# Attention, expert layer and MLP in one kernel: the short query chunk moved to the front, the start script rearranged, and its value products split into column halves

## The chip, the cores and the metric

The kernel runs on one core of one Trainium2 chip. The metric is the device time of one execution in microseconds. The time before is 407.12 us, the median of three runs (406.49 to 407.96).

The engines are called TensorE (PE in the rows; its weight loads are PEld), VectorE (DVE), ScalarE (ACT), GpSimd (POOL) and SyncE (SP), whose queue issues nearly all transfers.

## The reference

Three stages follow one another. The change touches only the first.

```python
scores = scale * np.matmul(q, k.transpose(0, 1, 3, 2))        # B=2, H=8, S=576, D=64
x = (psi_rel / psi_i)[..., None]                              # log-distance over log-position
bias = np.maximum(x @ w1 + b1, 0.0) @ w2                      # 32 hidden, one bias per head
attn = softmax(scores + bias.transpose(2, 0, 1)[None])
x = np.matmul(attn, v)                                        # to 1152 x 512 tokens
# then: top-1 mixture of 8 experts (512 -> 1024 -> 512) with a capacity,
# then: an MLP 512 -> 2048 -> 512 with a leaky ReLU
```

The bias depends on the position pair and the head, not on the batch.

## The kernel before, in words

**Chunks and units.** The 576 queries of a batch are cut into five chunks, 0 to 3 of 128 queries and chunk 4, the short one, of 64. A *unit* is one chunk of one batch for one pair of heads, so there are 40 units. `order` (L573) lists the ten (batch, chunk) pairs, and the units follow it, four head pairs each. Before, the first is (0, 1), chunk 1 of batch 0; the short chunk of batch 0 is the fifth.

In a full unit the two heads are two score tiles of 128 queries by 576 keys. In a short unit they share one: rows 0 to 63 are the one head, rows 64 to 127 the other.

**Bias groups.** The bias is made in 36 groups of 16 query rows. For a group, `relus` (L156) makes four ReLU tiles of D columns, D = max(16u + 16, 576 - 16u) for group u. Each goes to an engine by the letter that `RENG` (L62), picked by the digit in `RP` (L63), gives: D VectorE, A ScalarE, P GpSimd. `bias_mm` (L172) multiplies them by the second layer on TensorE, and evicts from PSUM with a scale: groups with D over 512 come in two pieces, the first evicted by VectorE and the second by ScalarE; the others in one piece, on the engine that `EP` (L64) names (1 is ScalarE). The result is stored to a scratch tensor in DRAM (`scr`), mirrored for both sides of the diagonal. `load_bias` (L300) reads a unit's bias back, shifted row by row. Groups are made in the order in which the chunks first appear in `order`. Chunk 2 has the narrowest groups (D 304 to 384), chunks 0 and 4 the widest (up to 576). `do_bias` (L593) makes the next group and then the ReLUs of the group two further on.

**The start script.** `START` (L58) is a list of words. `START[0]` is run first, then the ReLUs of two groups, and then, for each further entry, one bias group, its store, and the entry's words (L627 to L633). The words: Q loads the queries of the first or second chunk, q splits one pair's queries into a high and a low part, k loads the keys of a head pair, K splits them, v loads a part of the values, B loads biases up to a unit. Before, twelve groups are made before the first unit, and B3 stands behind the eighth. All loads go through the SP queue, which works in order; a bias load there waits until the stores of its chunk have landed. The keys of pairs 2 and 3 are split in `prep` (L645) of units 0 and 1: ScalarE casts, and by `KHE` (L61) GpSimd subtracts.

**The main loop** (L1265) runs iteration n as follows: scores of unit n+1 (`qk`, TensorE), transposes of unit n (`tr`), score reduction with the bias for unit n+1 (`ttr`, VectorE, once for each score tile), evictions of the transposes, exponentials of unit n+1 (`expo`, ScalarE), `prep` of later queries and keys, one bias group, the finishing steps of a chunk, value products of unit n-1 (`pv`, TensorE, L391), more bias groups, and bias loads up to unit n+5. `QUOTA` (L70) says how many groups iteration n makes: two in iterations 0 to 9, then one, so the last of 36 is made in iteration 13. The score tile has one buffer, the ReLU tiles of a group three. `PF` (L69) says in which iterations a piece of the sorted-token buffer is pre-filled (six transfers of 771 KB), and batch 1's keys are split in iterations 8 to 10, with a subtraction on VectorE (`k_late`, L273).

**Value products.** `pv` gives for each of five key tiles, in a full unit, one product per head: 64 weight columns (the head's values) by 128 moving columns (the queries), each written to its own 64 rows of the output. In a short unit it gives one product for both heads: 128 weight columns by 128 moving columns, of which the finishing step reads the two diagonal 64 by 64 blocks. Every float32 product appears in the trace as two matmul passes.

The expert stage and the MLP start when attention has ended. The main loop's order, cut:

```python
    for n in range(N + 1):
        if n + 1 < N:
            st = s0(n + 1)
        if n < N:
            tt = tr(units[n][1], At.pop(n))
        if n + 1 < N:
            sv = ttr(*units[n + 1][1:], st, bts[n + 1])
...
            At[n + 1] = expo(c, p, sv, rst[b, c])
            prep(n + 1)
        q = quota[n]
        if q:
            do_bias()
...
            pv(c, p, ATt.pop(n - 1), Vt[b], xpt[b, c])
...
        for _ in range(q - 1):
            do_bias()
```

## Time and profile before

| | us |
|---|---|
| median of three runs | 407.12 |
| the profiled execution | 408.05 |
| its span, first to last instruction | 406.3 |
| TensorE busy | 375.9 |
| VectorE busy | 307.7 |
| ScalarE busy | 242.9 |
| GpSimd busy | 139.1 |

The profiled execution took 408.05 us, of which 406.3 are its span. Attention fills about the first 210 us, the expert stage and the MLP the rest. In a timeline row stand the start in us, the time in us, the engine, the line, the operation with the tiles it writes and reads, the shape, and in brackets how long the engine was idle before it and what ended that. Rows of one kind that follow one another are merged (x8 is eight). A matmul's end is modelled, so the cost of a step on TensorE is read from its start to the start of the next row.

### The profile page before, as it was taken

To read this page: it belongs to the slowest core of one execution; us is meant where nothing else is said; L and a number is where in the kernel's file an instruction comes from. 1 tells how busy PE (TensorE), PEld (TensorE's weight loads), DVE (VectorE), ACT (ScalarE), POOL (GpSimd) and SP (SyncE) were. 2 spreads that over 40 slices of the span, in tenths; PEclk is the share of its full clock that TensorE was granted. 3 is DMA by queue.
4 is the path that set the end of the run, shared out by engine and by line. 5 is a ranking of instruction groups with operands and counts; after the bars stand their busy time and mean duration, and the time that the engine had idled before them with its cause. 6 is when DMAs were issued, how large, how long until landed. Compare 5 with 4: busy or idle time off the path is not lost. (4 is left out here: it accounts for less than half of the span.)

```text
span 406.3 us, 8427 instructions
## 1 busy us (share of the span) xinstructions
PE 375.9 (93%) x2990; PEld 312.6 (77%) x2990; DVE 307.7 (76%) x733; ACT 242.9 (60%) x522; POOL 139.1 (34%) x110
## 2 busy tenths in 40 slices
PE   4777999988999999999999999999999999899993
PEld 2234666756688888988889999998988778788872
DVE  5998989899854888899458972137899999999310
ACT  3857898788865878767654875556544222455100
POOL 1445857574101110212332206840242255222311
PEclk9999899999999999999998999999999999999997
DMA  7979599798879938889185299683243366530011
GB/s 180 320 235 322 157 330 313 274 297 250 216 236 262 353 135 233 224 253 250 46 236 201 69 327 343 217 289 114 106 173 127 106 207 206 209 106 2 19 59 51
DMA packets 34050, 81.79 MB, mean 201 GB/s; under 512 B 8427, under 2 KB 8811, under 8 KB 31952
## 3 DMA queue, kind: packets, MB, share of 16 engines
q1 hardware_dynamic: 32880, 78.70, 61.3%
q0 software_dynamic: 1120, 2.48, 1.7%
q8 instruction: 25, 0.41, 0.4%
q14 instruction: 25, 0.20, 0.2%
HBM read 59.11 MB, written 23.20 MB: 203 GB/s over the span
## 5 line engine op out<-in xcount | busy, mean ns | idle before, releaser
L341 DVE CUSTOM_DVE_ANT_0 sv<-St,bt 128x576 f32<-128x576 f32 x72 | 52.9, 750 | 30.8 <-PE St L329 18.8
L672 POOL TENSOR_TENSOR P<-raw,P 128x1024 fp32r<-128x1024 f32 x18 | 45.3, 2521 | 76.6 <-ACT P L671 63.5
L352 ACT ACTIVATE A<-sv,mx 128x576 f32<-128x576 f32 x72 | 59.3, 837 | 3.2 <-DVE mx L341 3.0
L329 PE MATMUL St<-K,Q 128*128 128x320 f32 (+1 forms) x320 | 53.6, 310 | 2.6 <-DVE mx L341 2.2
L329 PEld LDWEIGHTS St<-K,Q 128*128 128x128 f32 x320 | 43.9, 189 | 14.6 <-issue 8.4
L182 PE MATMUL pb<-Gt,WP 128*32 128x272 f32 (+17 forms) x352 | 42.1, 505 | 13.3 <-DVE Gt L165 7.5
L269 POOL TENSOR_TENSOR Q<-qr,Q 128x256 fp32r<-128x256 f32 x22 | 16.9, 769 | 99.9 <-ACT Q L261 62.1
L165 DVE TENSOR_SCALAR Gt<-WL,bp 128x400 f32<-128x400 f32 (+17 forms) x98 | 49.4, 563 | 0.1
L671 ACT CAST P<-raw 128x1024 fp32r<-128x1024 f32 x27 | 28.3, 1048 | 28.3 <-DVE raw L689 22.7
L362 PE MATMUL pt<-CS,A 128*128 128x128 f32 x288 | 41.5, 284 | 1.3 <-ACT A L352 0.8
L372 ACT COPY AT<-pt 128x512 f32<-128x512 f32 x40 | 23.3, 583 | 29.2 <-PE pt L362 28.9
L362 PEld LDWEIGHTS pt<-CS,A 128*128 128x128 f32 x288 | 38.1, 206 | 2.2 <-ACT A L352 1.3
L169 POOL TENSOR_SCALAR Gt<-WL,bp 128x528 f32<-128x528 f32 (+12 forms) x17 | 34.1, 2009 | 8.2 <-DVE Gt L165 7.3
L399 PE MATMUL xp<-AT,V 128*64 128x128 f32 x512 | 35.9, 284 | 0.0
L399 PEld LDWEIGHTS xp<-AT,V 128*64 128x64 f32 x512 | 28.0, 139 | 9.8 <-issue 9.5
L182 PEld LDWEIGHTS pb<-Gt,WP 128*32 128x32 f32 x352 | 12.4, 110 | 29.8 <-DVE Gt L165 14.7
L856 PE MATMUL g<-yhl,P 128*128 128x304 f32 x96 | 30.5, 318 | 3.9 <-DVE gfa L881 3.9
L193 ACT ACTIVATE bs<-pb,CS 128x288 f32<-128x288 f32 (+53 forms) x60 | 27.2, 500 | 10.1 <-PE pb L182 9.5
L1193 PE MATMUL ac<-P,hq 128*128 128x512 f32 (+1 forms) x80 | 31.5, 394 | 0.0
L1191 PE MATMUL ac<-P,hq 128*128 128x512 f32 (+1 forms) x80 | 31.5, 394 | 0.0
L1192 PE MATMUL ac<-P,hq 128*128 128x512 f32 (+1 forms) x80 | 31.5, 394 | 0.0
L889 DVE TENSOR_TENSOR hq<-gfa,hq 128x304 fp32r<-128x304 f32 x32 | 28.9, 902 | 1.4 <-ACT hq L888 1.4
(322 smaller groups left out, 907.4 us busy)
## 6 DMA issues: line engine op xcount, KB each, us to landing
bt<-scr SPq DMA_DIRECT2D x24, 576.0 KB, 6.0
w<-wo SPq DMA_DIRECT2D x13, 1024.0 KB, 5.0
scr<-bs SPq DMA_DIRECT2D x36, 295.5 KB, 4.2
raw<-wm SPq DMA_DIRECT2D x14, 512.0 KB, 6.2
w<-wm SPq DMA_DIRECT2D x10, 512.0 KB, 5.7
srt<-pre SPq DMA_DIRECT2D x6, 771.0 KB, 8.4
qr<-qc SPq DMA_DIRECT2D x16, 256.0 KB, 5.7
w64g<-wo SPq DMA_DIRECT2D x3, 1024.0 KB, 10.3
```

The costliest lines, as they stand in the source:

```text
L165: nc.vector.tensor_scalar(G, src, bp[:, g : g + 1], 0.0, op0=ALU.add, op1=ALU.max)
L169: nc.gpsimd.tensor_scalar(G, src, bp[:, g : g + 1], 0.0, op0=ALU.add, op1=ALU.max)
L182: nc.tensor.matmul(pb[32 * q : 32 * q + 32, 0 : hi - lo], W2, gs[:, q, lo:hi], start=True, stop=True)
L329: nc.tensor.matmul(St[:, o + lo : o + hi], Q[:, h - 2 * p, w, :], K[:, h - 2 * p, lo:hi], start=n == 0, stop=n == len(seq) - 1)
L341: nc.vector.tensor_tensor_reduce(out=sv, in0=St, in1=bt[:, jb], scale=-0.125, scalar=3.0e38, op0=ALU.add, op1=ALU.min, accum_out=mx)
L352: nc.scalar.activation(A[:, :, j], sv, AF.Exp, bias=mx, scale=-1.0, accum_out=rs[:, col : col + 1])
L362: nc.tensor.transpose(pt[:, 128 * t : 128 * t + 128], A[:, 128 * t : 128 * t + 128, j], ident)
L399: nc.tensor.matmul(xp[64 * j : 64 * j + 64, p, :], w, a, start=t == 0, stop=t == NFULL)
L672: eng.tensor_tensor(out=P_[:, 1], in0=raw, in1=P_[:, 0].bitcast(F32), op=ALU.subtract)
L1191: nc.tensor.matmul(ps, hh, wh, start=k == 0, stop=False)
L1192: nc.tensor.matmul(ps, hh, wl, start=False, stop=False)
L1193: nc.tensor.matmul(ps, hl, wh, start=False, stop=k == F2 // 128 - 1)
```

## The change

Six constants change, and two pieces of code:

- `order` begins with the short chunk, (0, 4), then (0, 2) and (0, 1). The bias groups follow: chunk 4 (four groups), 2, 1, 3, 0. Batch 1 still begins at unit 12.
- `START` makes eight groups instead of twelve, with the queries of both first chunks and the keys 0 and 1 loaded before the first; B3 stands behind the fourth group, the values and the keys 2 and 3 behind B3.
- `QUOTA` makes three groups in iterations 0 and 1 and two in each of 2 to 12, so the last is made in iteration 12.
- `RP`, `RENG`, `EP` put ReLUs and evictions of some groups on other engines: VectorE has 99 ReLUs instead of 98, ScalarE 29 as before, GpSimd 16 instead of 17.
- `PF` moves the first four pre-fills to iterations 8, 11, 14 and 17 (before 1, 3, 8 and 14).
- In `pv`, a short unit's product is made per head, 64 weight columns by that head's 64 moving columns.

```diff
-START = ["Q0 k0 k1", "q0 v0", "q1 K0 v1", "q2", "Q1 q3 v2", "", "K1", "k2", "v3 B3 k3", "", "", "", ""]
+START = ["Q0 k0 k1 Q1", "", "q0", "K0 q1", "B3 q2 q3 k2", "K1 v0 v1", "v2 v3 k3", "", ""]
-RENG = ('DAAA', 'DADD', 'DAPD', 'DDDD', 'DDPA', 'DDAD')
-RP = "355355535352525234144534444144444342"
-EP = "111111111100011111111101110111111111"
+RENG = ('DAAA', 'DADD', 'DAPD', 'DDDD', 'DDPA', 'DDAD', 'DADA')
+RP = "565633533353525234144534444144444342"
+EP = "111111111111111111111101110111111111"
-PF = (3, 8, 1, 14, 21, 28)
-QUOTA = [2, 2, 2, 2, 2, 2, 2, 2, 2, 2, 1, 1, 1, 1, 1, 1, 1, 1, 1, 1, 1, 1, 1, 1, 2, 2, 1, 1]
+PF = (8, 11, 14, 17, 21, 28)
+QUOTA = [3, 3] + [2] * 11
...
-            for t in range(NFULL):
-                nc.tensor.matmul(xp[:, p, :], V[:, t, 128 * p : 128 * p + 128], AT[:, 0, 128 * t : 128 * t + 128],
-                                 start=t == 0, stop=False)
-            nc.tensor.matmul(xp[:, p, :], vt[:, 128 * p : 128 * p + 128], AX_[0:64], start=False, stop=True)
+            for t in range(NFULL + 1):
+                for j in range(2):
+                    r = slice(64 * j, 64 * j + 64)
+                    h = slice(128 * p + 64 * j, 128 * p + 64 * j + 64)
+                    w, a = (V[:, t, h], AT[:, 0, 128 * t + 64 * j : 128 * t + 64 * j + 64]) if t < NFULL else (vt[:, h], AX_[0:64, r])
+                    nc.tensor.matmul(xp[r, p, r], w, a, start=t == 0, stop=t == NFULL)
...
-    order = [(0, 1), (0, 0), (0, 3), (1, 3), (0, 4), (0, 2), (1, 2), (1, 1), (1, 0), (1, 4)]
+    order = [(0, 4), (0, 2), (0, 1), (1, 1), (0, 3), (0, 0), (1, 0), (1, 3), (1, 2), (1, 4)]
```

## Rows read from the trace of the kernel before

**Rows 1.** Busy us by stretch: PE, PEld, DVE, ACT, POOL; clock, DMA share, GB/s.

```profile
10.00:20.00 10.00, 7.53 (x44) 2.18 (x37) 9.91 (x20) 8.89 (x19) 4.47 (x4) 1.00 1.02 319
...
40.00:50.00 10.00, 9.96 (x90) 5.83 (x90) 9.96 (x24) 8.33 (x20) 8.84 (x14) 0.83 0.50 155
```

**Rows 2.** Timeline of TensorE, a full unit: scores, transposes, value products, next scores.

```profile
165.89 1.34 PE L329 MATMUL St<-K,Q 128*128 128x320 f32 x8
167.07 1.11 PE L362 MATMUL pt<-CS,A 128*128 128x128 f32 x8
...
168.22 1.09 PE L399 MATMUL xp<-AT,V 128*64 128x128 f32 x16
169.14 0.39 PE L399 MATMUL xp<-AX__2356,vd 128*64 128x128 f32 x4
169.46 1.33 PE L329 MATMUL St<-K,Q 128*128 128x320 f32 x8
```

**Rows 3.** Timeline of TensorE, a unit of the short chunk.

```profile
131.22 1.32 PE L329 MATMUL St<-K,Q 128*128 128x320 f32 x8
132.38 0.63 PE L362 MATMUL pt<-CS,A 128*128 128x128 f32 x4
...
132.95 1.06 PE L402 MATMUL xp<-AT,V 128*128 128x128 f32 x8
...
134.39 1.29 PE L329 MATMUL St<-K,Q 128*128 128x320 f32 x8
```

**Rows 4.** Timeline of TensorE, a wide and a narrow bias group, each with its successor.

```profile
63.09 1.04 PE L182 MATMUL pb<-Gt,WP 128*32 128x496 f32 x8
64.05 0.66 PE L436 MATMUL px<-CS,xt 128*128 128x128 f32 x4
...
83.36 0.72 PE L182 MATMUL pb<-Gt,WP 128*32 128x304 f32 x8
84.01 1.34 PE L329 MATMUL St<-K,Q 128*128 128x320 f32 x8
```

**Rows 5.** Timelines: the first score reduction on VectorE; scores of unit 3 on TensorE.

```profile
29.54 0.74 DVE L341 CUSTOM_DVE_ANT_0 sv<-St,bt 128x576 f32<-128x576 f32 x1
...
44.77 1.34 PE L329 MATMUL St<-K,Q 128*128 128x320 f32 x8
```

**Rows 6.** Timeline of the start: the load of keys 3 and its use on ScalarE.

```profile
28.17 0.50 SPq L226 DMA_DIRECT2D kr<-kc  x1
...
37.46 1.15 ACT L235 CAST K<-kr 64x1152 fp32r<-64x1152 f32 x1 [2.28 <-DMA kr<-kc]
```

**Rows 7.** Timelines: ReLUs on VectorE, alone and beside GpSimd's key subtraction.

```profile
4.85 1.54 DVE L165 TENSOR_SCALAR Gt<-WL,bp 128x448 f32<-128x448 f32 x4
...
79.10 0.66 DVE L165 TENSOR_SCALAR Gt<-WL,bp 128x320 f32<-128x320 f32 x2
...
12.10 1.54 DVE L165 TENSOR_SCALAR Gt<-WL,bp 128x368 f32<-128x368 f32 x1
...
12.00 2.90 POOL L238 TENSOR_TENSOR K<-kr,K 64x576 fp32r<-64x576 f32 x2 [0.25 <-POOL Q L269]
```

**Rows 8.** Timeline of the SP queue: last store of the first chunk, its bias loads.

```profile
21.03 0.32 SPq L222 DMA_DIRECT2D scr<-bs  x1
...
25.21 2.86 SPq L310 DMA_DIRECT2D bt<-scr  x4
```

**Rows 9.** Timeline of TensorE: router products with 64 moving columns, and their successor.

```profile
141.31 0.32 PE L444 MATMUL pl<-xt,WP 128*32 128x64 f32 x8
141.56 1.09 PE L399 MATMUL xp<-AT,V 128*64 128x128 f32 x16
```

**Rows 10.** Timelines: a late TensorE hole, key subtractions of batch 1, evictions of a wide group.

```profile
87.72 0.72 PE L182 MATMUL pb<-Gt,WP 128*32 128x304 f32 x8 [1.30 <-ACT bs L193]
...
93.17 2.62 DVE L276 TENSOR_TENSOR K<-kr,K 64x1152 fp32r<-64x1152 f32 x2
...
79.68 0.65 DVE L195 TENSOR_SCALAR bs<-pb,CS 128x16 f32<-128x16 f32 x2
```

## The prediction

> **What bounds the kernel now.** I read the busy shares by stretch first, then TensorE's timeline, then the timelines of the other engines where TensorE has holes.
>
> By stretch: between 10 and 20 us VectorE is full and TensorE is not; between 40 and 50 us TensorE is full, at a granted clock of 0.83 on average [rows 1]. "Full" has to be checked, because a matmul's end is modelled. What does not lie is the distance from one start to the next. A full attention unit costs TensorE 1.18 us of scores, 1.15 of transposes and 1.24 of value products, in all 3.57 us [rows 2]. A unit of the short chunk costs 1.16 + 0.57 + 1.44 = 3.17 us [rows 3]. A bias group of width D costs 0.96 us at 496 columns and 0.65 at 304 [rows 4], so 0.16 + 0.0016 D.
>
> With these prices I count packed work. The first score reduction starts on VectorE at 29.54 us and the scores of unit 3 on TensorE at 44.77 [rows 5]. By then TensorE has done 16 bias groups (widths summing to 7296: 14.2 us), scores of three units (3.5), transposes of two (2.3), products of one (1.2): 21.3 us of work in 44.8, so 23.5 us are lost. From there to 111 us, where the last bias group ends, the same count leaves only about 4 us lost, all after 86 us, and from there to the end of attention nearly nothing. So the question for the change is **when TensorE becomes packed, how much work is then left, and whether it stays packed.**
>
> Why it starts late: VectorE works through the ReLUs of 14 bias groups before the first score reduction, and then ScalarE stands still for 2.28 us for the keys of pair 3, whose load was issued at 28.17 and used at 37.46, 9.3 us later [rows 6]. While it stands, bias evictions and ScalarE's ReLUs queue behind that key cast, and TensorE behind them.
>
> **The change part by part.**
>
> *Eight groups ahead, four of them for the first chunk.* By the strings, VectorE does 33 ReLUs before the first reduction instead of 44. One costs 0.37 us at 448 columns and 0.29 at 320 [rows 7], so 11 fewer are about 4.4 us: the first reduction moves from 29.5 to about 25. Its bias must be there too. The four wide groups need on VectorE 10 wide ReLUs (4.2 us), 4 narrow ones (1.2), 4 evictions of about 0.6 (2.4) and the split of one query pair, which I take at 0.6; from 4.85 that is 13.3 us. K0's subtraction on GpSimd falls into this: a ReLU beside it took 1.54 us instead of about 0.33 [rows 7], so 14.5. The last store of the old first chunk was issued at 21.03, and the bias load, which waits for its landing, at 25.21 [rows 8]; with the same 4.2 us the bias load goes out at 18.7 and the data is there by about 23. VectorE is later, so 25 stands.
>
> *Key loads.* Keys 0 and 1 stay where they were; the second chunk's queries move ahead of everything (two issues on SP at a moment when nothing waits, and a memset of the short queries on GpSimd, idle then: I cost these at nothing; if that cover went, the first store would be some 2 us later, 2 us of start). Keys 2 and 3 are behind the bias load on SP. The four issues of it took 2.86 us [rows 8], then come keys 2, two stores, seven issues of values, and keys 3: ten issues at about half a microsecond, so keys 3 go out near 26.5, two us earlier than before. When they land is the unknown: after 4.2 us if the queues are as idle as for that store [rows 8], after 9.3 us as before [rows 6]; as many bytes stand ahead of it (1.15 MB of bias and 1.25 MB of values, before 2.3 MB of bias), but spread over more time. I take 5.5 us, nearer to the idle end: 32 us.
>
> *From there to a packed TensorE.* Three groups in iteration 0 put group 10 ahead of the scores of unit 2 in TensorE's order, and one ReLU of group 10 lies on ScalarE behind the cast of keys 3. Cast 1.1, two evictions and the ReLU about 1.4: group 10 starts at 34.5. Then group 10 (0.75), scores (1.18), short transposes (0.57), groups 11 to 13 (0.77, 0.88, 0.85), one short product (0.9): the scores of unit 3 start at about 40, against 44.77. Bounds: 36 if keys 3 cost no wait, 44.3 if they land after 9.3 us.
>
> *Work left then.* Done by 40 us: 14 groups (widths 5776: 11.5), three scores 3.5, two short transposes 1.1, one short product 0.9, in all 17.1, that is 4.2 less than before at the same place.
>
> *Column halves.* Two heads share a 128-column product in the short chunk, of which half is never read. Now 20 passes of 64 weight columns by 64 moving columns stand for 10 passes of 128 by 128. No row shows such a pass. Upper bound: the 20 passes of a full unit, twice as many moving columns, 1.24 us [rows 2]. Lower bound: half of that, 0.62, which is also 20 times the 31 ns of a router product with 64 moving columns (eight in 0.25 us) [rows 9]. I take the middle, 0.9, since a narrower tile form next to a 128-wide one costs something at each border. It saves 0.54 of 1.44 per unit, 4.3 us over eight units (bounds 1.6 to 6.6). Four of them lie at the very end of attention, on a packed TensorE; the first four lie in the start and are already in the 0.9 above. [...]
>
> *Deferred groups.* 28 groups now lie in iterations 0 to 12, the wide ones of chunk 0 last, in iterations 8 to 12, where batch 1's keys are also split on VectorE (1.35 us each, four times) and TensorE already had its late holes, such as 1.30 us [rows 10]. VectorE there: 18 ReLUs of about 0.45 (8.1 us) instead of 14 of about 0.29 (4.1); eight eviction moves of wide groups, two per group in 0.65 [rows 10] or some 0.6 a group, 2.4, and one more group evicted by it, 0.8. That is 7.2 us more. TensorE: ten groups (10.5 us) instead of seven (4.9), 5.6 more. So VectorE's surplus over TensorE grows by 1.6 us; the wide GpSimd ReLUs may add one. I take 2.5; bounds 0 (VectorE runs ahead in iterations 2 to 7, where the narrow groups are) and 7.2 (all of it exposed).
>
> *Prefills* move from iterations 1, 3, 8 and 14 to 8, 11, 14 and 17: same bytes, same queue, hidden behind bias loads issued five units ahead; without that cover one load, 6 us once. Cost nothing. The other order of chunks changes nothing else by count: batch 1 starts at unit 12, the last chunk is the same.
>
> **The sum**, against the profiled execution's own 408.05 us: start −4.8; work left: 4.2 more for the start, 4.3 less for the halves, −0.1; late +2.5. Together −2.4: 405.65. That execution is 0.93 above the median of 407.12, so **404.7 us** on the median's scale.
>
> **The rivals.**
>
> *A, slower: VectorE becomes the bound in iterations 8 to 12.* All 7.2 us are exposed: −4.9 + 7.2 = +2.3, 409.4 us. It decides if VectorE is more than one iteration behind when iteration 9 begins. For: the holes there already, with less VectorE work. Against: units 0 to 3 need one reduction instead of two, which lets VectorE arrive earlier. Chance 0.26.
>
> *B, no change: keys 3 are as late as before.* Unit 3 starts at 44.3, −0.6 with the work left, and half of the late cost, 1.2: 407.7 us. For: as many bytes ahead; against: the earlier issue. Chance 0.12.
>
> *C, no change: the halves save 0.2 us per unit.* That takes back 2.7: 407.4. [...] Chance 0.08.
>
> *D, much faster: keys 3 cost no wait.* Unit 3 at 36, late cost 1: −7.9, 399.2 us. Chance 0.14.
>
> **How the numbers follow.** My forecast has 0.40, centred on 404.7, with its own range 402.0 to 406.0. Faster by over 0.3% (1.2 us, about what a measurement of this kernel can tell from no change): forecast and D, 0.54. Within: B and C, 0.20. Slower: A, 0.26. The range 400.0 to 409.4 cuts off half of D and about half of A's spread, some 0.2.
>
> **What the profile afterwards would show.** Right: first reduction near 25 us; scores of unit 3 near 40 with a ScalarE wait for keys 3 before it; short units' products 0.9 us from start to start; TensorE's holes after 70 us around 6 us instead of 4. Wrong: unit 3 at 44 (B); products at 1.2 (C); no wait for keys 3 (D); long VectorE releases ahead of the reductions between 75 and 110 us (A). It is also wrong if attention ends earlier but the expert stage behind it does not.

## The result, and the profile after

The change makes the kernel slower: a median of 412.0 us (411.58 to 414.75, four runs) against 407.54 for the kernel before (four runs), ratio 1.0118, 95% interval 1.0083 to 1.0153. A second set of six runs of the same changed kernel gave 415.6 us (412.71 to 416.51), ratio 1.0188 (1.0161 to 1.0214). The kernel before stays within 406 to 410, two slow executions of 1504 and 1963 us left out. That the changed kernel spreads over 5 us is part of the result.

The profiled execution took 412.36 us, 4.31 more than the profiled one of before. The rows that answer to [rows 3, 5, 6] come from the timelines of the start:

```profile
25.30 0.76 DVE L341 CUSTOM_DVE_ANT_0 sv<-St,bt 128x576 f32<-128x576 f32 x1 [0.63 <-PE St L329]
...
32.02 1.15 ACT L235 CAST K<-kr 64x1152 fp32r<-64x1152 f32 x1 [2.61 <-DMA kr<-kc]
...
34.52 1.44 PE L182 MATMUL pb<-Gt,WP 128*32 128x368 f32 x4 [1.11 <-ACT Gt L167]
35.89 2.29 PE L329 MATMUL St<-K,Q 128*128 128x320 f32 x8
37.98 0.71 PE L362 MATMUL pt<-CS,A 128*128 128x128 f32 x4
...
39.51 0.69 PE L406 MATMUL xp<-AT,V 128*64 128x64 f32 x16
40.12 0.33 PE L406 MATMUL xp<-AX__363,vt 64*64 64x64 f32 x4
40.38 2.05 PE L182 MATMUL pb<-Gt,WP 128*32 128x448 f32 x16
42.37 1.33 PE L329 MATMUL St<-K,Q 128*128 128x320 f32 x8
```

The first reduction is at 25.30 us, keys 3 (those of head pair 3) are there at 32.02, group 10 starts at 34.52: three steps as forecast. Then unit 2's scores take 2.09 us from start to start, where 1.18 is the packed price [rows 2], and unit 3's begin at 42.37, not at 40. A short unit's products cost 0.87 us (39.51 to 40.38), against 1.44 [rows 3].

Busy time by stretch (us, PE, PEld, DVE, ACT, POOL, clock, DMA share, GB/s): one stretch of the start, then iterations 9 to 11, where the changed kernel has batch 1's key splits and the wide groups. The last line is the sum of the same four stretches in the kernel before.

```profile
30.00:40.00 10.00, 7.24 (x45) 3.87 (x45) 6.40 (x17) 5.97 (x12) 6.76 (x4) 0.66 0.66 209
...
80.00:85.00 5.00, 4.28 (x37) 2.90 (x36) 4.94 (x12) 3.94 (x10) 4.78 (x2) 1.00 0.43 96
85.00:90.00 5.00, 4.87 (x61) 3.36 (x59) 4.97 (x10) 4.39 (x7) 4.99 (x4) 1.00 1.05 338
90.00:95.00 5.00, 2.49 (x33) 1.50 (x34) 4.97 (x12) 2.62 (x6) 0.85 (x2) 1.00 0.78 214
95.00:100.00 5.00, 5.00 (x57) 3.21 (x53) 4.97 (x13) 2.86 (x5) 4.73 (x3) 1.00 0.56 191
sum 20.00, PE 16.64 PEld 10.97 DVE 19.84 ACT 13.81 POOL 15.35; mean PE 4.16 PEld 2.74 DVE 4.96 ACT 3.45 POOL 3.84
```

```profile
sum 20.00, PE 17.49 PEld 12.69 DVE 19.68 ACT 17.55 POOL 11.95; mean PE 4.37 PEld 3.17 DVE 4.92 ACT 4.39 POOL 2.99
```

VectorE is full for all 20 us (19.84), TensorE is not (16.64). The full share alone proves little: in the kernel before VectorE was as full there (19.68), and its TensorE waits of 1.30, 0.50 and 0.47 us were ended by ScalarE. What is new is who ends the waits: the two of the changed kernel, 0.72 and 2.51 us, are ended by VectorE. Between 90 and 95 ScalarE and GpSimd stand too. The timelines of the three engines there show the order of the waits:

```profile
88.10 1.26 DVE L165 TENSOR_SCALAR Gt<-WL,bp 128x528 f32<-128x528 f32 x2
89.39 2.62 DVE L276 TENSOR_TENSOR K<-kr,K 64x1152 fp32r<-64x1152 f32 x2
92.04 0.76 DVE L341 CUSTOM_DVE_ANT_0 sv<-St,bt 128x576 f32<-128x576 f32 x1
...
92.84 0.81 ACT L352 ACTIVATE A<-sv,mx 128x576 f32<-128x576 f32 x1 [2.23 <-DVE mx L341]
...
94.14 0.33 PE L455 MATMUL pl<-CS,lt 128*128 128x128 f32 x1 [2.51 <-DVE AT L381]
```

Two ReLUs of a wide group and two key subtractions stand on VectorE ahead of unit 11's two reductions; ScalarE waits 2.23 us for the reduction, TensorE 2.51 us for the copy of transposes queued behind it. Two more holes are new, in stretches where the kernel before had none. Timelines of ScalarE, VectorE and TensorE:

```profile
120.49 0.30 ACT L471 ACTIVATE lg<-lg,tm 128x8 f32<-128x8 f32 x1 [1.26 <-DVE tm L469]
...
122.51 1.23 PE L362 MATMUL pt<-CS,A 128*128 128x128 f32 x8 [0.87 <-ACT A L352]
...
186.83 0.30 ACT L471 ACTIVATE lg<-lg,tm 128x8 f32<-128x8 f32 x1 [2.27 <-DVE tm L469]
...
187.56 0.35 DVE L487 TENSOR_TENSOR acc<-acc,oh 128x8 f32<-128x8 f32 x2
187.86 0.76 DVE L341 CUSTOM_DVE_ANT_0 sv<-St,bt 128x576 f32<-128x576 f32 x1
...
189.45 1.31 PE L329 MATMUL St<-K,Q 128*128 128x320 f32 x8 [1.79 <-DVE mx L341]
```

At 120 us the small exponential of the router (the step that picks a token's expert) waits on ScalarE, in order, for VectorE's chain of small steps, and holds up a unit's exponential. At 187 the routing counts are added up: the main loop derives from the chunk order when batch 1's counts are added, and the new order makes of one piece, at iteration 38, two, at 30 and 38. The first forces the whole router chain through VectorE ahead of a reduction.

Where the 4.31 us lie: for each stretch, the elapsed time less its work at the prediction's packed prices (the cost of a step from start to start), each against the kernel before. Start +1.8 lost; from unit 3 to unit 14 +1.6 lost; from unit 14 to the last product about +4.0 lost, 2.7 of it the two holes above; products −4.6 (8 times 0.57). Attention ends at 214.43 instead of 211.58, +2.85. Behind it TensorE waits 1.80 us for the sorted rows, before 0.35 (timelines of TensorE, the kernel before and then the one after):

```profile
240.52 0.66 PE L723 MATMUL g<-CS,xr 128*128 128x128 f32 x4 [0.35 <-DMA xr<-srt]
```

```profile
243.29 0.66 PE L725 MATMUL g<-CS,xr 128*128 128x128 f32 x4 [1.80 <-DMA xr<-srt]
```

2.85 and 1.45 make the 4.3.

### The profile page after: what moved, and what is told of

It is laid out like the page before. It is cut to its first block, busy times and chain, and to the rows that moved or that the text cites. A ratio compares the mean times of both kernels' runs of the same rounds, so it can differ in the third digit from the quotient of the medians.

```text
span 410.5 us, 8573 instructions
## 1 busy us (share of the span) xinstructions
PE 373.9 (91%) x3070; PEld 308.6 (75%) x3070; DVE 306.1 (75%) x732; ACT 245.0 (60%) x524; POOL 142.3 (35%) x109
## 5 line engine op out<-in xcount | busy, mean ns | idle before, releaser
L329 PEld LDWEIGHTS St<-K,Q 128*128 128x128 f32 x320 | 45.2, 194 | 17.4 <-issue 11.0
L182 PE MATMUL pb<-Gt,WP 128*32 128x264 f32 (+17 forms) x352 | 44.4, 524 | 14.4 <-DVE Gt L165 10.5
L329 PE MATMUL St<-K,Q 128*128 128x320 f32 (+1 forms) x320 | 54.6, 315 | 2.9 <-DVE mx L341 2.7
L269 POOL TENSOR_TENSOR Q<-qr,Q 128x256 fp32r<-128x256 f32 x22 | 20.8, 945 | 94.0 <-ACT Q L261 54.4
L165 DVE TENSOR_SCALAR Gt<-WL,bp 128x320 f32<-128x320 f32 (+17 forms) x99 | 44.9, 513 | 0.1
L169 POOL TENSOR_SCALAR Gt<-WL,bp 128x400 f32<-128x400 f32 (+12 forms) x16 | 33.9, 2123 | 3.2 <-PE pb L182 3.1
L399 PE MATMUL xp<-AT,V 128*64 128x128 f32 x512 | 35.0, 279 | 0.0
L193 ACT ACTIVATE bs<-pb,CS 128x272 f32<-128x272 f32 (+53 forms) x60 | 27.4, 505 | 10.1 <-PE pb L182 6.8
```

The lines of the kernel that those rows point to most:

```text
L165: nc.vector.tensor_scalar(G, src, bp[:, g : g + 1], 0.0, op0=ALU.add, op1=ALU.max)
L169: nc.gpsimd.tensor_scalar(G, src, bp[:, g : g + 1], 0.0, op0=ALU.add, op1=ALU.max)
L182: nc.tensor.matmul(pb[32 * q : 32 * q + 32, 0 : hi - lo], W2, gs[:, q, lo:hi], start=True, stop=True)
L329: nc.tensor.matmul(St[:, o + lo : o + hi], Q[:, h - 2 * p, w, :], K[:, h - 2 * p, lo:hi], start=n == 0, stop=n == len(seq) - 1)
L399: nc.tensor.matmul(xp[64 * j : 64 * j + 64, p, :], w, a, start=t == 0, stop=t == NFULL)
```

## The experiments

The experiments were timed in five sets, each beside 11 to 17 runs of the kernel before, whose median was 407.45 to 407.94. "Attention ends" is the end of the last value product in the profile; holes are TensorE's waits of 0.3 us and more from 44 us to there.

| kernel | median us (runs) | ratio, 95% | attention ends | holes |
|---|---|---|---|---|
| before | 407.5 | 1 | 211.6 | 3.9 |
| changed | 412.0 (4) | 1.0118 (1.0083 to 1.0153) | 214.4 | 7.5 |
| order_only | 415.47 (6) | 1.0215 (1.0184 to 1.0246) | 221.6 | 7.8 |
| halves_only | 407.34 (11) | 0.9988 (0.9971 to 1.0004) | 209.8 | 3.6 |
| no_halves | 414.95 (6) | 1.0190 (1.0162 to 1.0218) | 219.4 | 6.3 |
| kp_spread | 414.34 (5) | 1.0161 (1.0138 to 1.0184) | 216.8 | 8.2 |
| vec_relief | 412.22 (6) | 1.0126 (1.0087 to 1.0164) | 214.7 | 7.1 |
| kp_relief | 410.44 (6) | 1.0079 (1.0066 to 1.0092) | 212.9 | 5.4 |
| all6 | 406.71 (12) | 0.9970 (0.9952 to 0.9988) | 209.5 | 3.5 |
| all6_nohalves | 411.02 (5) | 1.0090 (1.0075 to 1.0104) | 211.2 | 3.0 |

### The parts of the change, alone

**halves_only**: the kernel before, with the new products.

```diff
-            for t in range(NFULL):
...
+            for t in range(NFULL + 1):
+                for j in range(2):
+                    r = slice(64 * j, 64 * j + 64)
...
```

> The kernel before, with only the value products of the short chunk in column halves. In the profile of the changed kernel a short unit's products take 0.87 us from start to start, before 1.44: 0.57 saved on each of eight units. Theory (the halves are a gain by themselves, and the loss comes from the schedule): all eight units lie on a packed TensorE in the old order, so up to 4.6 us less, 403 to 405 us. Rival (the halves are what costs, for instance by a change of tile form at each border that shows later): 407.5 us or more.

407.34 us: no change that could be told, though attention ended 1.8 us earlier in the profile. Less than 0.57 us a unit arrives: the last four units, from 199.74 to 211.58 before, ran from 199.49 to 209.80, 1.53 us saved in place of 2.28, and from unit 3's scores to the end of attention 2.3 us were saved in place of 4.6. Behind attention the waits for the sorted rows grew from 0.35 to 1.03 us.

**no_halves**: the changed kernel with the old products (the reverse of that diff).

> The changed kernel with the old 128 by 128 products in the short chunk; all else as changed. Theory (the halves gain, the schedule loses): slower than the changed kernel, by 2.3 us for the four last units and up to 1.7 for those at the front, 414 to 416 us. Rival (the halves cost): 408 to 411 us.

414.95 us, 3 more than the first set of the changed kernel and 0.6 less than the second: inconclusive, because the changed kernel itself spreads that far.

**order_only**: the kernel before, with the new order and nothing else.

```diff
-    order = [(0, 1), (0, 0), (0, 3), (1, 3), (0, 4), (0, 2), (1, 2), (1, 1), (1, 0), (1, 4)]
+    order = [(0, 4), (0, 2), (0, 1), (1, 1), (0, 3), (0, 0), (1, 0), (1, 3), (1, 2), (1, 4)]
```

> The kernel before with the new order of chunks alone: old start script (twelve groups ahead), old quota, old engines, old products. Theory (the order alone costs, by full units in the place where the short ones were, the earlier flush of the routing counts, and wide groups beside the key splits): 411 to 414 us. Rival (the start script and the quota are what costs): 407 to 409 us.

415.47 us: the order alone costs 8.0 us. The changed kernel in the same set (after_again, below) took 415.6, no less; what the rest of the change gives back lies within the spread (no_halves, 414.95, with all of it but the halves). The strings that pick engines go by position, so here they fall on other groups than they were written for: this is the order without a schedule made for it. The 8.0 also hold the wide groups beside the key splits, which the prediction had priced. The timeline of TensorE has the three large holes of the changed kernel, and behind the first the work runs at half speed (a full unit's products 2.33 us start to start, 1.24 in [rows 2]; granted clock 0.53 between 90 and 95 us):

```profile
90.95 1.11 PE L436 MATMUL px<-CS,xt 128*128 128x128 f32 x4 [2.52 <-DVE AT L381]
91.99 0.66 PE L444 MATMUL pl<-xt,WP 128*32 128x128 f32 x8
92.58 1.98 PE L399 MATMUL xp<-AT,V 128*64 128x128 f32 x16
94.34 0.64 PE L399 MATMUL xp<-AX__1047,vd 128*64 128x128 f32 x4
94.91 1.99 PE L182 MATMUL pb<-Gt,WP 128*32 128x264 f32 x16
...
128.58 1.23 PE L362 MATMUL pt<-CS,A 128*128 128x128 f32 x8 [0.90 <-ACT A L352]
...
195.13 1.29 PE L329 MATMUL St<-K,Q 128*128 128x320 f32 x8 [1.79 <-DVE mx L341]
```

**after_again**: the changed kernel once more, unchanged.

> The changed kernel once more, as it is, beside the others of this set on one chip, since its four runs so far spread over 3 us. Expected: 411.5 to 414 us, scores of unit 3 at 42 us, TensorE's holes of about 1 us near 121 and 1.8 us near 188 at the same places. If the holes after 110 us are at other places, they belong to single executions.

415.6 us. Its profile ended attention 3.0 us later than the first profile, with the same hole of 2.51 us. What differs is what follows it. TensorE's timeline, then the stretch by engine:

```profile
95.07 0.43 PE L455 MATMUL pl<-CS,lt 128*128 128x128 f32 x1 [2.51 <-DVE AT L381]
95.44 1.97 PE L399 MATMUL xp<-AT,V 128*64 128x128 f32 x16
97.20 0.64 PE L399 MATMUL xp<-AX__1134,vd 128*64 128x128 f32 x4
...
95.00:100.00 5.00, 4.93 (x43) 3.50 (x44) 3.65 (x13) 3.08 (x6) 3.40 (x3) 0.66 0.58 210
```

Granted clock 0.66 where the first profile had 1.00. From unit 11's scores to unit 12's it took 10.05 us instead of 8.48. Eight of the profiles have a hole of 2.5 us or more between 70 and 100 us; in four of them the clock then falls (0.53 to 0.79 in the 5 us stretch at the hole's end in three, 0.83 between 70 and 80 us in kprep_early), in four it stays at 1.00. That is one source of the spread; the start was 0.9 us later as well.

### The start

**keys3_early**: the changed kernel, keys 3 loaded one step earlier.

```diff
-START = ["Q0 k0 k1 Q1", "", "q0", "K0 q1", "B3 q2 q3 k2", "K1 v0 v1", "v2 v3 k3", "", ""]
+START = ["Q0 k0 k1 Q1", "", "q0", "K0 q1", "B3 q2 q3 k2", "K1 k3 v0 v1", "v2 v3", "", ""]
```

> The changed kernel with the load of keys 3 issued directly behind keys 2, ahead of the values. Theory (ScalarE's 2.6 us wait for keys 3 holds up group 10 and with it the scores of unit 2, and TensorE's hole then halves its clock): no wait on ScalarE, scores of unit 3 near 38 us instead of 42.4, and 3 to 4 us of it kept: 408 to 409 us. Rival (VectorE is the bound until the bias is done): scores of unit 3 earlier, but the holes in iterations 8 to 12 grow by as much: 411 to 412 us.

412.27 us, ratio 1.0113 (1.0093 to 1.0133). ScalarE's wait is gone, yet unit 3's scores moved only from 42.37 to 41.87. The timelines of GpSimd, VectorE and TensorE show what was late next:

```profile
27.86 5.83 POOL L238 TENSOR_TENSOR K<-kr,K 64x576 fp32r<-64x576 f32 x4 [1.08 <-issue]
...
28.12 1.31 DVE L263 CAST Q<-qr 128x256 fp32r<-128x256 f32 x1
29.46 1.50 DVE L266 TENSOR_TENSOR Q<-qr,Q 128x256 fp32r<-128x256 f32 x1
30.89 5.73 DVE L165 TENSOR_SCALAR Gt<-WL,bp 128x368 f32<-128x368 f32 x10
...
32.49 0.81 PE L182 MATMUL pb<-Gt,WP 128*32 128x368 f32 x2 [3.42 <-DVE Gt L165]
```

Beside GpSimd's four subtractions a query cast took VectorE 1.31 us, elsewhere 0.28, and the split's subtraction 1.50, elsewhere 0.42. So the ReLUs behind them are late, and TensorE waits 3.42 us for those. TensorE's granted clock, which the expectation speaks of, was 0.50 from 32 to 38 us in the changed kernel: it had fallen by the end of a wait of 2.28 us for a ReLU of VectorE (to 31.66), ahead of the one of 1.11 that the late keys brought (to 34.52).

**keys_dve**: that kernel, with the subtractions of keys 2 and 3 on VectorE.

```diff
-KHE = "ADAA"
+KHE = "ADDD"
```

> As keys3_early, and the subtractions of keys 2 and 3 on VectorE instead of GpSimd. In keys3_early ScalarE's wait was gone, but GpSimd subtracted from 27.9 to 33.7 us and VectorE's query ops and the ReLUs of group 10 beside it took 2 to 4 times their time, so the scores of unit 2 came at 35.6 as before. Theory (the two key subtractions on GpSimd hold VectorE, and through group 10 TensorE): four VectorE ops of 0.7 us instead, group 10 at about 31 us, scores of unit 2 near 32 and of unit 3 near 37 to 38, and 3 to 4 us of it kept: 408 to 409 us. Rival (the start is given back in iterations 8 to 12, where VectorE is the bound): scores of unit 3 as early, unit 14 no earlier than 108, 411 to 412 us.

413.51 us, ratio 1.0157 (1.0129 to 1.0184); unit 3's scores at 42.35. VectorE's timeline:

```profile
28.05 1.42 DVE L238 TENSOR_TENSOR K<-kr,K 64x576 fp32r<-64x576 f32 x2 [1.80 <-ACT K L235]
...
30.39 0.28 DVE L263 CAST Q<-qr 128x256 fp32r<-128x256 f32 x1
...
32.27 1.42 DVE L238 TENSOR_TENSOR K<-kr,K 64x576 fp32r<-64x576 f32 x2 [1.15 <-DMA vd<-vc]
33.70 3.46 DVE L165 TENSOR_SCALAR Gt<-WL,bp 128x368 f32<-128x368 f32 x10
```

With GpSimd idle there, the same cast took 0.28 us again and ten ReLUs 3.46 in place of 5.73: the subtractions on GpSimd were what slowed them. But nothing was won. The four subtractions now took VectorE 2.84 us, and it stood 1.80 and 1.15 us ahead of them, while ScalarE cast the keys (the second cast ended at 32.24). So the ten ReLUs were done at 37.16, against 36.62 in keys3_early.

**halves_k23**: the old order with the halves, keys 2 and 3 loaded earlier, keys 2 split in the start.

```diff
-START = ["Q0 k0 k1", "q0 v0", "q1 K0 v1", "q2", "Q1 q3 v2", "", "K1", "k2", "v3 B3 k3", "", "", "", ""]
+START = ["Q0 k0 k1", "q0 v0", "q1 K0 v1", "q2 k2", "Q1 q3 v2", "", "K1 k3", "", "v3 B3", "K2", "", "", ""]
```

> The kernel before in its old order with the column halves, head pair 2's key load issued four steps earlier and head pair 3's two steps earlier in the start, and head pair 2's split done in the start. If the late keys set the start in the old order, as GpSimd's end of the split at 37.0 us just before unit 2's scores at 37.7 us says, unit 3's scores come 1.5 to 4 us earlier than the 45.3 us of the halves alone, and the time is 404.5 to 406.5, below both kernels. If the ReLU rows of the bias groups set it (VectorE is busy without a break from 24 to 32 us) or the wait for the sorted rows takes the gain up, the time is 406.5 to 408.

412.02 us, ratio 1.0095 (1.0065 to 1.0125), a clear miss. GpSimd's subtraction now stood ahead of its own ReLUs for the groups, and TensorE waited for those; unit 3's scores came at 50.41 in place of 45.29. Timelines of GpSimd and TensorE:

```profile
25.38 2.97 POOL L238 TENSOR_TENSOR K<-kr,K 64x576 fp32r<-64x576 f32 x2 [9.47 <-ACT K L235]
28.45 4.36 POOL L169 TENSOR_SCALAR Gt<-WL,bp 128x528 f32<-128x528 f32 x2
...
30.94 1.98 PE L182 MATMUL pb<-Gt,WP 128*32 128x264 f32 x12 [3.07 <-POOL Gt L169]
32.85 2.29 PE L329 MATMUL St<-K,Q 128*128 128x320 f32 x8
```

### Iterations 8 to 12

**kprep_early**: the changed kernel, batch 1's keys loaded and split two to three iterations earlier.

```diff
-VL, KL, KP = ((9, 9, 13, 12), (8, 9, 9, 10), (9, 10, 10, 11))
+VL, KL, KP = ((9, 9, 13, 12), (5, 6, 7, 8), (6, 7, 8, 9))
```

> The changed kernel with batch 1's keys loaded and split three iterations earlier (iterations 5 to 8 instead of 8 to 10), where the narrow groups are. Theory (wide groups and key splits fall together on VectorE in iterations 8 to 10 and give the holes near 84 and 93 us): those holes shrink, scores of unit 14 at 107 us or earlier instead of 108.7, 410.5 us. Rival (VectorE is as full in iterations 5 to 7): the holes move forward, 412 us.

413.25 us, ratio 1.0136 (1.0120 to 1.0153). The hole at 94 went and another came at 71 to 75, of 3.56 us: a key load, one iteration ahead of its cast as in the changed kernel, was late here, and the cast stood 4.23 us on ScalarE for it, with all that was queued behind it. ScalarE's timeline, then TensorE's:

```profile
72.11 1.15 ACT L232 CAST K<-kr 64x1152 fp32r<-64x1152 f32 x1 [4.23 <-DMA kr<-kc]
...
74.68 0.99 PE L182 MATMUL pb<-Gt,WP 128*32 128x464 f32 x8 [3.56 <-ACT bs L193]
```

So this run tested another wait than the one meant.

**kp_spread**: the loads two iterations ahead, the splits one to an iteration.

```diff
-VL, KL, KP = ((9, 9, 13, 12), (8, 9, 9, 10), (9, 10, 10, 11))
+VL, KL, KP = ((9, 9, 13, 12), (6, 7, 8, 9), (8, 9, 10, 11))
```

> The changed kernel with batch 1's four key loads two iterations ahead of their splits (6, 7, 8, 9) and the splits one to an iteration (8, 9, 10, 11), where two fell into iteration 10. Theory A: the two key subtractions of 1.31 us each that stand together on VectorE ahead of the reductions make the 2.51 us hole of TensorE at 92 to 94 us, and where that hole is long the granted clock falls to half behind it. Then the hole shrinks to under 1.3 us, iterations 11 to 12 take 7 us or less in place of 8.5 to 10, the attention ends 1.3 to 3 us earlier than 214.4 to 217.5, and the time is 410 to 413 with less spread than the changed kernel's 411.6 to 416.5. Rival B: VectorE is full from iteration 8 to 12 whatever the place of the splits, because chunk 0's wide groups are made beside them; the hole moves to another iteration and the time stays at 412 to 416.

414.34 us. The holes of 0.72 and 2.51 became 1.81 and 1.57: 3.2 before, 3.4 after. VectorE stayed at 19.87 of 20 us, and the granted clock was 1.00 from 80 to 100 us in both profiles: that it falls behind a long hole was seen in after_again (0.66) and not behind the 2.51 us of the first profile. That is the rival: the hole moves.

**vec_relief**: the changed kernel, one ReLU row moved from VectorE to ScalarE in five wide groups; in a sixth, three leave VectorE, two for ScalarE and one for GpSimd.

```diff
-RENG = ('DAAA', 'DADD', 'DAPD', 'DDDD', 'DDPA', 'DDAD', 'DADA')
-RP = "565633533353525234144534444144444342"
+RENG = ('DAAA', 'DADD', 'DAPD', 'DDDD', 'DDPA', 'DDAD', 'DADA', 'DAPA')
+RP = "5656335333535252341445344441777777""42"
```

> The changed kernel with one of VectorE's two ReLU rows given to ScalarE in six of the widest bias groups (those made in iterations 8 to 10): pattern DAPA in place of DDPA (one group DDDD), 0.7 us less on VectorE for each group, some 1.4 us in each of three iterations. Theory A, VectorE is the bound in iterations 8 to 12 because the new order makes chunk 0's wide groups beside batch 1's key splits: the two holes of TensorE there (0.72 and 2.51 us) shrink to under 1.5 us together, the attention ends 1.5 to 3 us earlier, and the time is 410 to 413. Rival B, ScalarE in its own order is as late as VectorE (key casts of 1.15, exponentials): the holes keep their sum of 3.2 us or grow and the time stays at 412 to 416.

412.22 us. VectorE's busy time from 80 to 100 us fell by 2.1 us to 17.76, TensorE gained 0.6 of it, and the holes became 0.92, 0.63 and 1.24. Neither theory's number for the holes, and a time that fits both: the load went down, and the two subtractions in one iteration kept a hole.

**kp_relief**: both edits together.

> The changed kernel with two edits together, the key splits one to an iteration and six wide groups with one ReLU row moved from VectorE to ScalarE; neither alone moved its time (414.3 and 412.2). Theory A, the two are surpluses on one engine of which each alone suffices to make the hole: together the holes of TensorE between 80 and 100 us fall from 3.2 us to about 1.5 us, and the time is 409 to 411. Rival: what made the kernel with everything fast (406.7) is the accumulation in one piece and the earlier key load, and this one stays at 412 to 414.

410.44 us (409.89 to 411.27). The holes are 0.64 and 0.80. The sums of the stretches from 80 to 100 us, each from its own kernel: kp_spread, vec_relief, kp_relief.

```profile
sum 20.00, PE 16.62 PEld 11.41 DVE 19.87 ACT 14.11 POOL 14.70; mean PE 4.15 PEld 2.85 DVE 4.97 ACT 3.53 POOL 3.68
```

```profile
sum 20.00, PE 17.21 PEld 11.73 DVE 17.76 ACT 18.70 POOL 15.49; mean PE 4.30 PEld 2.93 DVE 4.44 ACT 4.67 POOL 3.87
```

```profile
sum 20.00, PE 18.56 PEld 12.31 DVE 17.64 ACT 19.22 POOL 16.39; mean PE 4.64 PEld 3.08 DVE 4.41 ACT 4.81 POOL 4.10
```

TensorE did 16.62, 17.21 and 18.56 us of work, at a granted clock of 1.00 in all of them, against 16.64 in the changed kernel. Less load alone gave 0.6, spreading alone nothing, both 1.9. Now ScalarE is at 19.22, which leaves little room to move more there.

**narrow_last**: the changed kernel with chunks 0 and 2 exchanged in both batches, so that the narrow groups come last, as before.

```diff
-    order = [(0, 4), (0, 2), (0, 1), (1, 1), (0, 3), (0, 0), (1, 0), (1, 3), (1, 2), (1, 4)]
+    order = [(0, 4), (0, 0), (0, 1), (1, 1), (0, 3), (0, 2), (1, 2), (1, 3), (1, 0), (1, 4)]
```

> The changed kernel with chunk 0 in place of chunk 2 behind the short chunk and chunk 2 in place of chunk 0 at the end of batch 0, so that the wide groups (464 to 576 columns) come first and the narrow ones (304 to 384) beside batch 1's key splits, as in the kernel before. Theory A, what costs is where the wide groups stand: the holes from 84 to 95 us (3.2 us in the changed kernel) fall under 1 us, while the start grows by 1 to 3 us for four wide groups in place of four narrow ones; time 410 to 414. Rival C, the order costs through the full units in iterations 16 to 19 and the pairing of the chunks in the second half alone: the holes before 110 us stay at over 2.5 us, and the time is 414 to 418.

411.64 us, ratio 1.0095 (1.0062 to 1.0127). Unit 3's scores came 3.8 us later (46.16), and attention still ended 0.5 us earlier than in the changed kernel: no hole over 1 us is left, the largest are 0.92 and 0.90, and those from 84 to 95 us sum to 0.8, as theory A had it. Two things went at once, though. In this order chunk 0 of batch 1 comes late, so the routing counts are added in one piece again, and the hole of 1.79 us is gone for that reason. What was won behind unit 3 was given back in the start.

**halves_kp**: the old order with the halves, splits spread as in kp_spread.

> The kernel before in its old order, with the column halves and with the same spreading of batch 1's key splits. If the splits in one iteration cost in the old order too (its holes from 87 to 106 us sum to 3.9 us, most of them ended by ScalarE's or VectorE's copies), 1 to 2 us of them go and the time is 405.5 to 407, below the kernel before. Rival: the old order has narrow groups there and the copies are late for want of ScalarE; the time is that of the halves alone, 407.3, within 0.5 us.

408.69 us, ratio 1.0022 (1.0004 to 1.0040): slower, if anything. The spread splits met other work, a router exponential that stood 2.96 us on ScalarE for VectorE's chain, and a hole of 1.58 us came at 79. What helps in one order is not an improvement by itself.

### The accumulation, and all together

**acc_late**: the changed kernel, batch 1's routing counts in one piece.

```diff
-    ACCN, m = [], NB0 + 6
+    ACCN, m = [], 38
```

> The changed kernel with the accumulation of batch 1's routing counts queued in iteration 38 for all chunks, as it fell out in the old order; in the changed order chunks 0 and 1 of it fall due in iteration 31, where the flush also forces the whole routing chain of a chunk onto VectorE ahead of a score reduction. Theory: TensorE's hole of 1.8 us at 187 us goes, 410 to 410.5 us. Rival (the hole belongs to the one profiled execution, or the work comes back later): 412 us.

414.44 us (411.11 to 416.12), ratio 1.0169 (1.0149 to 1.0189). In the profile, which was the fastest of the five runs, the hole at 189 us is gone and attention ends 1.6 us earlier; the median says nothing of it, being inside the changed kernel's own spread.

**kp_acc**: kp_spread and acc_late.

> The same as the run before it, and the accumulation of batch 1's routing counts in one piece at iteration 38 in place of two at 30 and 38. Theory A with the accumulation as a cause of its own: the 1.8 us hole at 189 us goes as well, the attention ends about 1.6 us earlier than in the run before it, and the time is 0.5 to 1.5 us lower than there, the rest being taken up by the wait for the sorted rows behind the attention. Rival: the time saved at the end of the attention is all taken up by that wait, and the time equals that of the run before it within 0.5 us.

413.5 us, ratio 1.0148 (1.0118 to 1.0178), 0.8 under kp_spread, on overlapping ranges.

**all5**: that, with keys3_early.

> The run before it, and the load of head pair 3's keys issued one step earlier in the start. If the three causes (late key load, splits in one iteration, accumulation in two pieces) add, the time is 408 to 411, about that of the kernel before (407.5). If GpSimd and VectorE beside each other set the start whatever the load, as the earlier look at this edit showed (unit 2's scores at 35.6, unit 3's at 41.9), it is within 0.6 us of the run before it.

411.89 us, ratio 1.0093 (1.0067 to 1.0119). Unit 3's scores at 40.97, against 42.4 to 43.7 in the profiles of the changed order without the earlier load (narrow_last and order_only apart); with the same start they came at 41.87 in keys3_early and 42.13 in all6, so the load alone does not set them.

**all6**: that, with vec_relief.

> The changed kernel with all that was tried and seemed to help: earlier load of head pair 3's keys, key splits one to an iteration, one accumulation at iteration 38, and six wide groups with one ReLU row moved from VectorE to ScalarE. If VectorE is the bound in iterations 8 to 12, 1.5 to 3 us under the same without the last part (411.9), 409 to 410.5; if not, 411.5 to 413.5.

406.71 us (405.42 to 408.16), lower than forecast by either theory, and 0.3% under the kernel before (interval 0.9952 to 0.9988). Of the 4.4 us between its profile and that of all5, 1.75 lie before the end of attention and 2.6 behind it, where the two kernels do not differ. The holes from 44 us to the end of attention are 3.5 us, and the one at 92 is a third of what it was. TensorE's timeline:

```profile
92.11 0.33 PE L455 MATMUL pl<-CS,lt 128*128 128x128 f32 x1 [0.80 <-DVE AT L381]
```

**all6_nohalves**: that, with the old products.

> The fastest version so far (406.7) with the old value products for the short chunk, eight units of 1.44 us in place of 0.87 us. If the stages are bound by TensorE there, all of 8 x 0.57 = 4.6 us comes back at the end of the attention and 2 to 4.6 us of it in the time (409 to 411). If the saving is taken up as it was in the old order (0.5 us of it left), 406.7 to 408.

411.02 us: with the other mends in place the halves are worth 4.3 us in the medians, against 0.5 in the old order. The profiles do not show the difference on TensorE's path through attention: attention ends 1.7 us earlier with the halves here (211.2 to 209.5) and 1.8 earlier in the old order. What the profiles show of it (3.2 us here, 0.4 in the old order) lies behind attention, in the stretch up to the last instruction, which is 1.1 us shorter with the halves here (the waits for the sorted rows went from 1.47 to none) and was 1.3 longer in the old order (0.35 to 1.03). Why is open; the expectation of 4.6 us at the end of attention did not come true.

## Why the prediction was wrong, point by point

It said 404.7 us, faster. It is 412.0, outside the range of 400.0 to 409.4. Against the profiled execution the miss is 6.7 us (405.65 forecast, 412.36 measured). By its terms:

- **The step that failed: "The other order of chunks changes nothing else by count."** By count that holds, by time it does not: behind unit 14 the changed kernel lost about 4.0 us more than before, and the order alone cost 8.0 us. The step priced the order only where bias groups are made. The same loop also takes from it which kind of unit stands beside the router's steps (full ones in iterations 16 to 19, where the short ones were: 0.87 us at 122) and when the routing counts are added (1.79 at 189). The second is shown: the hole goes in every kernel that adds the counts in one piece. The first is argued: the hole is in every profile of the new order and in none of the old one at that place (the kernel before has a smaller one of its kind, 0.67 us, ahead of unit 14), but no run moves those units alone. Of the 4.0, 2.7 are these two holes; for 1.3 no single place was found.
- **The start, mis-sized by 2.4 us.** Steps one to three held to within half a microsecond. From group 10's start to unit 3's scores 7.85 us went by, not 5.5; the prediction's own prices for that stretch add up to 5.9, so 0.4 was lost in its sum. TensorE ran at a mean clock of 0.66 between 30 and 40 us, which the packed prices left out: group 10 took 1.37 us in place of 0.75 and unit 2's scores 2.09 in place of 1.18, 1.5 us together. And the key wait was not alone: keys3_early took it away, TensorE then waited 3.42 us for VectorE's ReLUs, and 0.5 us was won. The row for that was there: [rows 7] has a ReLU slowed beside GpSimd's key subtraction, and the prediction counted it for the keys of pair 0 and not for those of pairs 2 and 3.
- **Column halves: the price came out.** 0.87 us a unit against 0.9, so 4.6 us of work for 4.3. The 0.9 was the middle of two bounds and not read from a row, so that it lies so near is partly luck. That a border of tile forms costs something fits the rows: in a full unit the last four products take 0.32 us to the start of the next scores and the sixteen ahead of them 0.92, 0.23 for four [rows 2]; in a short unit now it is 0.26 against 0.15 (0.61 for sixteen). The 20 passes took 43 ns each, and rival C, which stood at the upper bound of 1.24 us, fell with that. That all of the saving arrives was wrong: in the profiles 1.7 to 1.8 us of it reached the end of attention, in the old order and in all6 alike, and the medians then differ by 0.5 and 4.3 us.
- **Deferred groups: the wait was right, its size within a microsecond.** 2.5 us were forecast between units 3 and 14, and 1.6 measured in the profile. But the hole has a second price that no term had: in four of the eight profiles with such a hole the clock falls behind it (to means of 0.53 to 0.83), and in after_again the way from unit 11 to unit 12 took some 1.5 us longer with it.
- **"It is also wrong if attention ends earlier but the expert stage behind it does not"**: attention ended later, and the wait for the sorted rows added another 1.45 us. Over all profiles the time from the end of attention to the last instruction was 192.0 to 198.0 us, the wait 0 to 2.1 of it, and it is shortest in the two profiles in which attention ends last (order_only and no_halves). So a gain at the end of attention can't be carried over to the time at face value.

These sum up: 2.4 − 0.9 + 4.0 − 0.3 + 1.45 = 6.65 of the 6.7. They must, since each stretch's loss is its elapsed time less its priced work; only the holes named in it are seen in rows.

Rival A named the wait that the runs then showed, TensorE held by VectorE in iterations 9 to 11, but not its size: it had 7.2 us exposed, and 1.6 were lost between units 3 and 14. That its 409.4 us comes nearest to the 412.0 is luck, since more was lost behind unit 14 than there. The sign "TensorE's holes after 70 us around 6 us" also came out by luck: they sum to 6.6, and 2.7 of that are the two holes that it had not priced. Rival B and rival D did not happen: keys 3 landed at 32.02 us, where the forecast had them.

How far the mends account for it: all6's profile took 406.58 us, 5.8 less than the changed kernel's. Attention ends 4.9 us earlier (214.43 to 209.50), of which 4.1 are holes: 1.8 the accumulation, 1.8 the two holes of iterations 9 to 11 (3.23 to 1.46), 0.75 at 105 us, 0.5 at 59, less 0.7 of two new small ones. Each mend alone stayed inside the changed kernel's own spread; the two on VectorE's load together (kp_relief, 410.44) did not. The other 0.9 us of the 5.8 lie behind attention.

What stays open: what decides whether the clock falls behind a hole, what else makes the changed kernel's executions differ by 5 us, and why the time behind attention differs by up to 6 us between kernels that do the same there. No run sets the clock by itself, and the quota, the pre-fills and the engine strings were not tried one by one.

## What to carry to other kernels

An order of tiles is also a schedule of everything hooked to it: before moving it, list each step whose place is derived from it, and ask which engine it lands on and what stands in that engine's queue. Here one engine was full over a stretch (VectorE, 19.84 of 20 us), and moving its work about only moved the hole; less work there and an even spread were both needed, and either alone looked useless. A saving on one engine has no worth of its own: the same 0.57 us a unit was 0.5 us of time in one schedule and 4.3 in another, so measure it again in the schedule that it will live in, and look at the stages behind it too.

## What was not expected of the hardware

The same hole of 2.5 us was followed by full speed in one execution and by half speed in the next (granted clock 1.00 and 0.66 between 95 and 100 us), and with that unit 12's scores began 8.48 or 10.05 us after unit 11's. And operations of 0.28 to 0.42 us on VectorE each took about as long as one of GpSimd's key subtractions beside them, although the two engines work on different tiles. In keys3_early a query cast took 1.31 us (alone 0.28) and the split's subtraction 1.50 (0.42), beside four subtractions of 5.83 us together. In the changed kernel the two took 1.32 and 1.50, beside subtractions of 1.42 and 1.44 us, and the ends go in turn: the cast ended at 29.75 us, just behind the first subtraction (29.60), the split's subtraction at 31.28, behind the second (31.00). A copy out of PSUM beside the first subtraction, at 28.23, took its usual 0.28 us. The slow ReLU of [rows 7] fits this too (1.54 us beside two subtractions of 2.90 together). That the times lay so near the neighbour's operation, at 4.7 times the own time of the cast and 3.6 times that of the split's subtraction, was not expected.
